# RWKV attention and two expert layers: r scaled in one piece, the diagonal term by transposed rows on TensorE, v loaded twice, decays on ScalarE, in the first two groups

## The chip, the cores and the metric

One core of a Trainium2 chip. The metric is device microseconds (us) of one execution; times of several runs of the kernel before: 460.25, 461.29 and 461.44, median 461.29. VectorE, ScalarE, GpSimd, TensorE and SyncE stand in the profile as DVE, ACT, POOL, PE and SP.

## What is computed

Three layers in a row, for 2 batches (B) of 768 tokens (S) of 384 values (8 heads H of D = 48). The change lies in the first, a linear attention with a state per head:

```python
def _attn_ref(r, k, v, w, u):
    B, H, S, D = r.shape
    state = np.zeros((B, H, D, D))
    for t in range(S):
        kt, vt, rt = k[:, :, t], v[:, :, t], r[:, :, t]
        cur = np.einsum('bhd,bhe->bhde', u[None] * kt, vt)
        y[:, :, t] = np.einsum('bhd,bhde->bhe', rt, state + cur)
        state = w[None, :, :, None] * state + np.einsum('bhd,bhe->bhde', kt, vt)
```

The term of `cur` (the diagonal term) is v of the same token times a coefficient, c = sum over d of r * u * k, one number per token and head. The second layer normalises each token and adds relu(x @ w_ch1) @ w_ch2 (384 to 1536 to 384). The third sends each token to one of 8 experts and multiplies with that expert's two matrices.

## The kernel before

**Groups.** Each batch is worked through in 6 groups g of 128 tokens. A group of batch b has the attention steps below; after them its tokens are normalised, transposed and pass the second layer's matmuls, and later routing to experts. Batch 1 goes a little ahead of batch 0 in the first two groups. After the sixth group the experts follow, one after another.

**An order written out by hand.** The string `ORDER` lists all steps; `name:engine.args` (p is POOL, d DVE, a ACT), for instance `kt:p.1.1` is step kt of batch 1, group 1 on GpSimd. The steps are issued in that order, so each engine, SyncE with its loads too, works through its own part of the list in order and waits wherever a step's input isn't there.

**Attention steps** of batch b, group g. Two blocks of 64 tokens (c = 0, 1) per group:
- `ld_T` (L256) loads r and k with heads' values on the partitions (r_, k_, 128 x 512); `ld_k` (L260) loads k with tokens on the partitions (kn_, 128 x 384); `ld_v` (L264) loads r that way (rn_), and v into two halves of the tile R.
- `kt` (L345) is k_ times powers of the decay; `L` (L348) is r_ times powers of it, for c = 0 and 1 in two calls of 64 partitions each; `knt` (L352) is kn_ times a table.
- `at` (at_pe, L383): 16 matmuls kt x L into a bank of PSUM; `am` (at_m, L391): on VectorE, two pieces, masks the result into L.
- The diagonal term: `rka` (L355) rn_ * u, `rkb` (L358) rn_ * kn_, `c` (L361) sums each head's 48 values (on ScalarE 8 pieces with an accumulator read each), `cv` (L369), in two halves, multiplies v (in R) with c.
- The state: `u` (u_pe, L398) 16 matmuls knt x v; `us` (u_s, L409) gives the state after the first block, a copy on ScalarE for group 0 and a sum on VectorE after; `uw` (L427) decays it; `ss` (s_s, L430) adds for the second block; `sw` (s_w, L433) decays that for the next group. `decayed` (L416) is one instruction on VectorE or GpSimd, and eight (one per head) on ScalarE.
- `y` (y_pe, L436): 16 matmuls; `yx` (y_x, L444) adds cv and sums; then `ym`, `yq`, `yr`, `ln` (L449 to L463) normalise (yr is on GpSimd always), `lt` (L466) transposes on TensorE, `lh` and `ll` (L471, L475) split the result into a high part and a residue.

**Weights of the second layer**, in the first stretch only: 12 chunks f. `ld_c.f` (L271) loads 768 KB into one of three tiles wq; `dec0`, `dec1`, `dec2` (L276 to L286) on VectorE decode a chunk to 32 bit; `w_g`, `w_hi` (L289, L294) on ScalarE scale it and round it to the high part, `w_lo` (L297) subtracts for the residue. With these, `m1.n` (mm1, L485) makes 18 matmuls for two chunks, `hh`, `hl` (L498, L501) take the relu apart on ScalarE and VectorE, `m2` (mm2, L508) makes 6 matmuls per batch. `SEQ` (L40) gives which two chunks m1.n needs: m1.0 the first two, m1.6 the last two (f = 10, 11).

Of the kernel before, what the change touches and what calls it, by code (L numbers as in the profile page):

```python
# [65 lines left out]
knt:d.1.3 yx.1.2 hh.11 rd.1.0 rl.0 hl.11 yr.0.2 knt:d.0.3 rm:d.0 m2.0.10 yq.1.2 yr.1.2 ln:p.0.2 rn.0 lt.0.2 rc.0 arg.0 ym:a.1.2
ln:p.1.2 lt.1.2 rkb:p.1.3 lh.0.2 lh.1.2 ll.0.2 m2.0.11 ll.1.2 ex.0 cv:p.0.3.0 L:p.0.3.1 x2.0.1 L:p.1.3.1 m2.1.11 x2.1.1 ld_v.0.4
row.0 m1.12 rr.0 hh.12 scan.0 col.0 L:d.1.3.0 oh.0 m1.13 hh.13 sum.0 hl.12 m2.1.12 rank.0 m1.14 pos.0 m2.0.12 c:d.1.3 hh.14
cv:p.0.3.1 hl.13 hl.14 m2.1.13 m2.0.13 ld_v.1.4 ld_k.1.4 m2.1.14 m2.0.14 sw:p.1.2 at.0.3 am.0.3 ld_T.0.4 cv:p.1.3.1 m1.15 hh.15
u.0.3 val.0 rw.0 tab.0 add.0 ld_k.0.4 m1.16 sw:a.0.2 us.0.3 hl.15 at.1.3 rka:p.0.4 m2.1.15 rt.0.1 uw:d.0.3 ss.0.3 y.0.3  # L70
rkb:p.0.4 c:a.0.4 ld_v.0.5 am.1.3 u.1.3 knt:p.1.4 yx.0.3 xs.0.1 us.1.3 uw:d.1.3 hh.16 yq.0.3 cv:p.0.4.1 re.0.1 ss.1.3 m1.17
xs.1.1 rt.1.1 y.1.3 hl.16 rd.0.1 re.1.1 ym:a.0.3 rd.1.1 m2.1.16 cv:p.1.3.0 yx.1.3 yq.1.3 hh.17 rka:d.0.5 hl.17 rl.1 m2.0.15
rm:a.1 rn.1 yr.0.3 sw:a.0.3 m2.0.16 ln:p.0.3 lt.0.3 rc.1 ym:p.1.3 arg.1 L:d.0.4.0 yr.1.3 ln:p.1.3 ld_T.1.4 L:p.1.4.1 lt.1.3
L:d.1.4.0 row.1 lh.0.3 lh.1.3 ll.0.3 rr.1 scan.1 ll.1.3 m2.1.17 x2.1.2 xs.1.2 m2.0.17 x2.0.2 rka:p.1.4 col.1 oh.1 m1.18 hh.18
L:d.0.4.1 hl.18 rank.1 m1.19 hh.19 sw:p.1.3 m2.1.18 rkb:p.1.4 pos.1 m2.0.18 hl.19 m2.1.19 ex.1 sum.1 val.1 m2.0.19 m1.20 c:d.1.4
ld_v.1.5 kt:d.0.4 hh.20 m1.21 rw.1 knt:p.0.4 hl.20 m2.0.20 ld_k.0.5 cv:d.0.4.0 m2.1.20 rkb:d.0.5 tab.1 hh.21 hl.21 kt:p.1.4
m2.1.21 c:a.0.5 ld_k.1.5 rka:p.1.5 rt.0.2 add.1 at.1.4 re.0.2 rd.0.2 am.1.4 rt.1.2 re.1.2 rd.1.2 cv:p.1.4.0 m2.0.21 cv:d.1.4.1
at.0.4 rl.2 rm:a.2 m1.22 am.0.4 u.0.4 hh.22 us.0.4 uw:p.0.4 u.1.4 rn.2 rc.2 ld_T.0.5 us.1.4 m1.23 hh.23 ss.0.4 y.0.4 kt:p.0.5
uw:d.1.4 ss.1.4 y.1.4 hl.22 hl.23 L:p.0.5.0 yx.0.4 yq.0.4 arg.2 ex.2 yx.1.4 yr.0.4 ym:d.0.4 L:d.0.5.1 ln:d.0.4 yq.1.4 ym:a.1.4
m2.0.22 row.2 rr.2 scan.2 m2.0.23 xs.0.2 x2.0.3 m2.1.22 lt.0.4 yr.1.4 ln:d.1.4 lt.1.4 lh.0.4 rkb:d.1.5 sum.2 lh.1.4 sw:p.1.4  # L80
m2.1.23 cv:p.0.5.1 ld_T.1.5 rt.0.3 col.2 ll.0.4 at.0.5 knt:p.1.5 x2.1.3 ll.1.4 m1.24 L:p.1.5.0 am.0.5 hh.24 hl.24 oh.2 m1.25
knt:p.0.5 re.0.3 m2.1.24 xs.1.3 rt.1.3 xs.0.3 rank.2 m1.26 u.0.5 cv:d.0.5.0 rd.0.3 hh.25 hl.25 val.2 re.1.3 L:p.1.5.1 rd.1.3
rl.3 pos.2 rw.2 tab.2 c:d.1.5 add.2 m2.1.25 hh.26 kt:p.1.5 at.1.5 m2.0.24 sw:p.0.4 us.0.5 am.1.5 y.0.5 rm:d.3 rn.3 rc.3 arg.3
u.1.5 m2.0.25 us.1.5 hl.26 row.3 yx.0.5 rr.3 scan.3 y.1.5 col.3 yq.0.5 m2.0.26 oh.3 rank.3 ym:a.0.5 cv:p.1.5.1 cv:p.1.5.0 yx.1.5
ym:a.1.5 yq.1.5 yr.0.5 ln:d.0.5 yr.1.5 ln:p.1.5 m1.27 lt.0.5 lh.0.5 pos.3 chp choose lt.1.5 lh.1.5 ll.0.5 m2.1.26 m1.28 ll.1.5
ldtop hh.27 hl.27 m2.1.27 ex.3 hh.28 hl.28 m2.0.27 m1.29 m2.0.28 sum.3 m2.1.28 hh.29 hl.29 m2.0.29 x2.0.4 m2.1.29 x2.1.4 rt.0.4
m1.31 re.0.4 val.3 rw.3 rd.0.4 xs.0.4 rt.1.4 m1.30 hh.31 hl.31 re.1.4 rd.1.4 rl.4 fill.4 fill.1 fill.3 hh.30 hl.30 fill.5 rm:a.4
fill.8 m1.33 rn.4 m1.32 rc.4 arg.4 row.4 m2.0.30 fill.6 hh.33 ex.4 sum.4 rr.4 scan.4 col.4 hl.33 tab.3 m2.1.30 oh.4 val.4 add.3
rank.4 pos.4 m2.0.31 fill.9 rw.4 m1.35 xs.1.4 hh.32 hl.32 fill.11 tab.4 fill.7 add.4 epc early eg.1 eg.0 m2.1.31 hh.35 fill.0
fill.10 m2.0.32 m1.34 m2.0.33 fill.2 lw.0 hh.34 hl.34 m2.1.32 hl.35 m2.0.34 m2.0.35 x2.0.5 m2.1.33 m2.1.34 etab m2.1.35 close  # L90
lw.1 x2.1.5 rt.0.5 re.0.5 ext.0 exh.0 rd.0.5 rt.1.5 xs.1.5 exl.0 re.1.5 rd.1.5 ext.1 exh.1 exl.1 rl.5 rm:d.5 e1.1 f0.2 f0.10
zX.0 rn.5 rc.5 arg.5 e1.0 row.5 f0.7 f0.1 f0.9 f0.8 f0.11 ex.5 sum.5 e1.2 e1h.1 e1l.1 rr.5 scan.5 col.5 e1h.0 e1l.0 oh.5 val.5
rank.5 pos.5 e1h.2 e1l.2 e1.3 e1h.3 e2.0.0 rw.5 e1l.3 pk finn tab.5 e2.0.1 add.5 fini f0.6 e2o.0 f0.4 f0.0 f0.3 xs.0.5 get.0.0
get.1.0 get.0.1 f0.5 f1.2 e2.1.0 e2.1.1 e2o.1 xt0.0 xh0.0 xl0.0 zX.1 f1.5 f1.0 lw.2 f1.1
f1.3 e2s.0 f1.4 e2s.1
# [1059 lines left out]
```

## Time and profile before

| | |
|---|---|
| median of three runs | 461.29 us (460.25 to 461.44) |
| the profiled execution's own time | 465.3 us |
| its span, first to last instruction | 463.4 us |
| busy: PE, DVE, POOL, ACT | 395.0, 308.5, 194.2, 186.3 us |
| mean granted clock of TensorE | 0.964 |

The rows used below come from views of one profiled execution. A row of stretches gives the stretch, its length, then per engine the busy us and the count of instructions (x), the granted clock (PEclk, share of full speed), the DMA engines' busy share and GB/s. A row of instructions in order of time gives start, length (of all, where several alike are merged as xN), engine, line, operation, output<-inputs, shape, and in brackets the idle time before it with what ended it. A row of groups gives the count, the summed busy us, the mean ns of one, and the idle before.

### The profile page before, as it was taken

The numbers are of one execution on the slowest core, as the hardware profiler recorded it, in microseconds if no ns is written. First come the engines' busy times: TensorE is split into PE (matmuls) and PEld (weight loads), VectorE is DVE, ScalarE is ACT, GpSimd is POOL, SyncE is SP. The second block draws the span as 40 slices with busy tenths as digits, with TensorE's granted clock in tenths as the row PEclk, the third lists the DMA queues.
The fourth block names the chain that finished last, engine by engine and source line by source line (L and its number), as shares of the span: only waits on it lengthen the run. The fifth ranks groups of instructions, "written<-read, shape, count | busy, mean of one in ns | idle before, by whom it ended". The sixth has DMA issues, their size and how long they took to land. (4 is left out here: it accounts for less than half of the span.)

```text
span 463.4 us, 8772 instructions
## 1 busy us (share of the span) xinstructions
PE 395.0 (85%) x3297; PEld 360.3 (78%) x3297; DVE 308.5 (67%) x606; ACT 186.3 (40%) x447; POOL 194.2 (42%) x252
## 2 busy tenths in 40 slices
...
GB/s 250 295 183 238 68 225 184 0 43 187 35 2 115 75 41 46 148 4 35 1 104 206 1 215 395 17 324 158 121 353 170 57 294 311 33 149 21 10 23 15
DMA packets 24849, 59.70 MB, mean 129 GB/s; under 512 B 3994, under 2 KB 10598, under 8 KB 24512
## 3 DMA queue, kind: packets, MB, share of 16 engines
...
q14 instruction: 43, 0.35, 0.2%
...
## 5 line engine op out<-in xcount | busy, mean ns | idle before, releaser
L514 PE MATMUL banks<-wh,H 128*128 128x384 f32 x288 | 84.9, 356 | 8.0 <-DVE H L502 6.5
L146 DVE TENSOR_TENSOR w2l<-wb,w2h 128x1024 fp32r<-128x1024 f32 (+1 forms) x33 | 33.1, 1028 | 52.9 <-ACT w2h L141 52.9
L514 PEld LDWEIGHTS banks<-wh,H 128*128 128x128 f32 x288 | 54.6, 196 | 10.3 <-DVE H L502 7.5
L973 PE MATMUL banks<-w1h,xq 128*128 128x512 f32 x168 | 58.3, 408 | 3.8 <-PEq L1060 2.8
L995 PE MATMUL banks<-w2h,H 128*128 128x384 f32 x224 | 48.2, 349 | 7.7 <-ACT H L141 7.7
L499 ACT ACTIVATE H<-banks 128x512 fp32r<-128x512 f32 x36 | 21.3, 594 | 78.7 <-PE banks L495 73.5
L514 PE MATMUL banks<-wl,H 128*128 128x384 f32 x144 | 50.0, 347 | 0.0
L995 PEld LDWEIGHTS banks<-w2h,H 128*128 128x128 f32 x224 | 40.9, 196 | 8.8 <-ACT H L141 8.2
L495 PE MATMUL banks<-xq,wh 128*128 128x256 f32 x216 | 44.7, 305 | 0.4 <-DVE xq L478 0.4
L973 PEld LDWEIGHTS banks<-w1h,xq 128*128 128x128 f32 x168 | 31.6, 188 | 13.6 <-issue 3.0
L495 PEld LDWEIGHTS banks<-xq,wh 128*128 128x128 f32 x216 | 36.8, 207 | 1.1 <-DVE xq L478 0.6
L502 DVE SCALAR_TENSOR_TENSOR H<-banks,H 128x512 fp32r<-128x512 f32 x36 | 24.5, 685 | 17.6 <-ACT H L499 17.5
L973 PE MATMUL banks<-w1l,xq 128*128 128x512 f32 x84 | 33.5, 398 | 0.2 <-DVEq L1060 0.2
L146 DVE TENSOR_TENSOR w1l<-wa,w1h 128x512 fp32r<-128x512 f32 (+1 forms) x36 | 32.5, 955 | 0.0
L495 PE MATMUL banks<-xq,wl 128*128 128x256 f32 x108 | 32.3, 299 | 0.0
L495 PE MATMUL banks<-xuh,wh 128*128 128x256 f32 x108 | 31.3, 290 | 0.0
L495 PE MATMUL banks<-xul,wh 128*128 128x256 f32 x108 | 30.6, 284 | 0.4 <-DVE xul L478 0.4
L495 PE MATMUL banks<-xuh,wl 128*128 128x256 f32 x108 | 30.5, 282 | 0.0
L141 ACT ACTIVATE w2h<-wb 128x1024 fp32r<-128x1024 f32 (+1 forms) x33 | 28.4, 902 | 3.2 <-DMA wb<-in_w 3.2
L372 POOL TENSOR_TENSOR cv<-R,c 64x384 f32<-64x384 f32 x19 | 18.8, 991 | 23.7 <-DVE c L367 22.0
L514 PEld LDWEIGHTS banks<-wl,H 128*128 128x128 f32 x144 | 28.2, 196 | 0.0
L141 ACT ACTIVATE w1h<-wa 128x512 fp32r<-128x512 f32 (+1 forms) x36 | 28.1, 855 | 0.0
...
## 6 DMA issues: line engine op xcount, KB each, us to landing
...
```

Source lines behind the costliest of these rows:

```text
L141: ACT.activation(out=dst_hi, in_=src, func=ACTF.Relu if relu else ACTF.Copy)
L146: (lo_eng or DVE).tensor_tensor(out=dst_lo, in0=src, in1=dst_hi.bitcast(F32), op=ALU.subtract)
L372: e.tensor_tensor(out=r3(cv[b][s], NH), in0=r3(R[b][g % 2][s, q, :], NH), in1=bc(c[s], [64, NH, HD]), op=ALU.mult)
L495: PE.matmul(out=ph[:, i, :], lhsT=a, rhs=x_[:, k, :], start=(q == 0), stop=(q == 8))
L499: ACT.activation(out=hh[:, ring(n)], in_=r3(B[3 + n % 2], 2), func=ACTF.Relu)
L502: DVE.scalar_tensor_tensor(out=hl[:, ring(n)], in0=r3(B[3 + n % 2], 2), scalar=0.0, in1=hh[:, ring(n)].bitcast(F32), op0=ALU.max, op1=ALU. ...
L514: PE.matmul(out=bank_o(b, g), lhsT=a[:, f2, s][:, i], rhs=w_[:, 2 * p + i, DM:], start=(p + i + n == 0), stop=(p == NP - 1 and i == 1 and ...
L973: PE.matmul(out=B[n], lhsT=a_[:, k, t], rhs=w_[:, k, n * 512:n * 512 + 512], start=(last == 0 and q == 0), stop=(last == 1 and q == KD - 1))
L995: PE.matmul(out=B[4][:, 0:DM], lhsT=a_[:, k, 0:128], rhs=w_[:, k, :], start=(q == 0), stop=(q == 23))
```

## The change

For groups 0 and 1 only: r times the powers is made in one piece (`Lr`, 128 partitions, into Ls); at_pe reads Ls, and ScalarE copies the two pieces that y_pe needs into L (`Lc`). The diagonal coefficient is made from the transposed rows: `rk` multiplies r_ by k_ in place, `cp` makes 16 matmuls of r_ with a column of u each, into the bank that at_pe used, and `cw` multiplies v with that column from PSUM. For that v is loaded into rn_ as well, in place of r. rka, rkb, c and cv of these groups go. All uw and sw of these groups are on ScalarE; w_lo, knt, kt, ln of the first stretch that stood on GpSimd are on VectorE, and five steps of group 2 as well (two L, two rka, one rkb; kt too). ld_un moves behind ld_v.0.1. Ls and two small tiles share the memory of x2. From cv.1.2.0 on the order is the old one. The order up to there and all other edits:

```diff
--- before.py
+++ after.py
@@ -33,7 +33,7 @@
 CAP = NTOK
 GATE_T = -1.5 * 2.0 ** -23
 BIG = float(1 << 20)
-C_ID, C_MK, C_RV, C_FT, C_JT, C_IO, C_TI, C_EO, C_JH, C_NC = 0, 128, 192, 200, 204, 220, 348, 360, 361, 385
+C_ID, C_MK, C_RV, C_FT, C_JT, C_IO, C_TI, C_EO, C_JH, C_UT, C_NC = 0, 128, 192, 200, 204, 220, 348, 360, 361, 385, 393
...
@@ -43,56 +43,55 @@
 
 ORDER = """
-zeros ld_wt zR:p.0.0 powers zR:p.1.0 ld_T.1.0 table kt:d.1.0 zR:p.0.1 ld_c.0 decay ld_cs L:d.1.0.1 L:d.1.0.0 zR:p.1.1 ld_gt wkc
-wkt wkn at.1.0 ld_T.0.0 L:p.0.0.1 ld_v.1.0 ld_un dec0.0 L:p.0.0.0 dec1.0 dec2.0 ld_k.1.0 knt:p.1.0 kt:d.0.0 ld_c.1 rka:d.1.0
-at.0.0 rkb:p.1.0 w_g.0 w_hi.0 w_lo:p.0 am.1.0 u.1.0 dec0.1 dec1.1 dec2.1 c:a.1.0 w_g.1 cv:d.1.0.1 ld_k.0.0 knt:p.0.0 w_hi.1
-us.1.0 am.0.0 ld_v.0.0 u.0.0 rka:p.0.0 rkb:d.0.0 c:a.0.0 us.0.0 uw:a.0.0 cv:p.1.0.0 ld_c.2 dec0.2 dec1.2 dec2.2 uw:d.1.0 ss.1.0
-y.1.0 w_g.2 ld_T.1.1 y.0.0 w_lo:p.1 ld_c.3 L:d.1.1.0 kt:p.1.1 yx.1.0 yq.1.0 ld_c.4 w_hi.2 cv:p.0.0.0 dec0.3 dec1.3 L:p.1.1.1
-cv:p.0.0.1 yx.0.0 yq.0.0 yr.1.0 at.1.1 ym:d.1.0 ym:p.0.0 ln:p.1.0 lt.1.0 yr.0.0 ln:p.0.0 ld_k.0.1 knt:p.0.1 dec2.3 ld_v.0.1
-w_lo:d.2 dec0.4 ss.0.0 dec1.4 dec2.4 w_g.3 w_hi.3 ld_v.1.1 lt.0.0 ld_k.1.1 lh.0.0 lh.1.0 w_g.4 w_hi.4 ll.0.0 w_lo:p.3 ld_T.0.1
-ll.1.0 L:p.0.1.1 u.0.1 m1.0 ld_c.5 kt:p.0.1 L:p.0.1.0 dec0.5 dec1.5 dec2.5 w_g.5 w_lo:d.4 rka:d.1.1 sw:p.0.0 ld_c.6 dec0.6
-rka:p.0.1 hh.0 rkb:p.0.1 dec1.6 w_hi.5 ld_c.7 hl.0 us.0.1 m1.1 hh.1 w_lo:p.5 dec2.6 hl.1 m2.0.0 m2.1.0 knt:p.1.1 dec0.7 dec1.7
-m2.0.1 dec2.7 uw:p.0.1 ss.0.1 w_g.6 ld_c.8 w_hi.6 w_lo:p.6 am.1.1 ld_c.9 dec0.8 m2.1.1 dec1.8 c:a.0.1 rkb:p.1.1 w_g.7 at.0.1
-am.0.1 w_hi.7 c:a.1.1 ld_c.10 m1.2 dec2.8 ld_k.1.2 w_g.8 hh.2 ld_k.0.2 w_lo:p.7 u.1.1 sw:p.1.0 m1.3 us.1.1 cv:p.1.1.0 cv:p.0.1.0
-hh.3 w_hi.8 cv:p.1.1.1 dec0.9 dec1.9 hl.2 y.1.1 yx.1.1 dec2.9 yq.1.1 ym:a.1.1 y.0.1 cv:p.0.1.1 yx.0.1 yq.0.1 uw:p.1.1 consts
-m2.1.2 hl.3 m2.0.2 w_g.9 w_hi.9 ym:d.0.1 m2.1.3 yr.1.1 ln:p.1.1 ss.1.1 lt.1.1 w_lo:d.8 yr.0.1 ln:d.0.1 dec0.10 ld_T.0.2 ld_c.11
-lt.0.1 lh.0.1 m2.0.3 kt:p.0.2 w_lo:d.9 m1.5 sw:d.1.1 lh.1.1 ll.0.1 ll.1.1 m1.4 dec1.10 dec2.10 ld_T.1.2 kt:p.1.2 hh.5 L:p.1.2.1
-hl.5 m2.1.5 m2.0.5 hh.4 dec0.11 w_g.10 w_hi.10 dec1.11 hl.4 m2.1.4 dec2.11 ld_v.0.2 w_g.11 rka:p.0.2 w_hi.11 rkb:p.0.2 m2.0.4
-L:p.0.2.1 c:d.0.2 m1.7 hh.7 ld_v.1.2 rka:p.1.2 rkb:d.1.2 w_lo:d.11 w_lo:p.10 m1.6 sw:d.0.1 hl.7 hh.6 hl.6 c:d.1.2 m2.0.7
-cv:p.1.2.0 ld_v.1.3 m2.1.7 m2.1.6 x2.1.0 xs.1.0 m2.0.6 x2.0.0 m1.8 hh.8 hl.8 L:p.1.2.0 xs.0.0 m1.9 hh.9 hl.9 cv:p.0.2.0
...
+zeros ld_wt zR:p.0.0 powers zR:p.1.0 ld_T.1.0 table kt:d.1.0 zR:p.0.1 ld_c.0 decay ld_cs Lr:d.1.0 zR:p.1.1 ld_gt wkc wkt wkn
+at.1.0 Lc.1.0.0 Lc.1.0.1 ld_T.0.0 Lr:d.0.0 ld_v.1.0 dec0.0 dec1.0 dec2.0 ld_k.1.0 knt:d.1.0 kt:d.0.0 ld_c.1 at.0.0 Lc.0.0.0
+Lc.0.0.1 rk:d.1.0 w_g.0 w_hi.0 am.1.0 cp.1.0 u.1.0 dec0.1 dec1.1 w_lo:d.0 dec2.1 w_g.1 ld_k.0.0 knt:d.0.0 w_hi.1 us.1.0 am.0.0
+ld_v.0.0 u.0.0 rk:d.0.0 cp.0.0 us.0.0 uw:a.0.0 cw:d.1.0 ld_c.2 dec0.2 dec1.2 dec2.2 uw:a.1.0 ss.1.0 y.1.0 w_g.2 ld_T.1.1 y.0.0
+w_lo:d.1 ld_c.3 Lr:d.1.1 kt:d.1.1 yx.1.0 yq.1.0 ld_c.4 w_hi.2 dec0.3 dec1.3 cw:d.0.0 yx.0.0 yq.0.0 yr.1.0 at.1.1 Lc.1.1.0
+Lc.1.1.1 ym:d.1.0 ym:d.0.0 ln:d.1.0 lt.1.0 yr.0.0 ln:d.0.0 ld_k.0.1 knt:d.0.1 dec2.3 ld_v.0.1 ld_un w_lo:d.2 dec0.4 ss.0.0
+dec1.4 dec2.4 w_g.3 w_hi.3 ld_v.1.1 lt.0.0 ld_k.1.1 lh.0.0 lh.1.0 w_g.4 w_hi.4 ll.0.0 w_lo:d.3 ld_T.0.1 ll.1.0 Lr:d.0.1 u.0.1
+m1.0 ld_c.5 kt:d.0.1 dec0.5 dec1.5 dec2.5 w_g.5 w_lo:d.4 sw:a.0.0 ld_c.6 dec0.6 hh.0 rk:d.0.1 dec1.6 w_hi.5 ld_c.7 hl.0 us.0.1
+m1.1 hh.1 w_lo:d.5 dec2.6 hl.1 m2.0.0 m2.1.0 knt:d.1.1 dec0.7 dec1.7 m2.0.1 dec2.7 uw:a.0.1 ss.0.1 w_g.6 ld_c.8 w_hi.6 w_lo:d.6
+am.1.1 ld_c.9 dec0.8 m2.1.1 dec1.8 rk:d.1.1 cp.1.1 w_g.7 at.0.1 Lc.0.1.0 Lc.0.1.1 am.0.1 cp.0.1 w_hi.7 ld_c.10 m1.2 dec2.8
+ld_k.1.2 w_g.8 hh.2 ld_k.0.2 w_lo:d.7 u.1.1 sw:a.1.0 m1.3 us.1.1 hh.3 w_hi.8 cw:d.1.1 dec0.9 dec1.9 hl.2 y.1.1 yx.1.1 dec2.9
+yq.1.1 ym:a.1.1 y.0.1 cw:d.0.1 yx.0.1 yq.0.1 uw:a.1.1 consts m2.1.2 hl.3 m2.0.2 w_g.9 w_hi.9 ym:d.0.1 m2.1.3 yr.1.1 ln:d.1.1
+ss.1.1 lt.1.1 w_lo:d.8 yr.0.1 ln:d.0.1 dec0.10 ld_T.0.2 ld_c.11 lt.0.1 lh.0.1 m2.0.3 kt:d.0.2 w_lo:d.9 m1.5 sw:a.1.1 lh.1.1
+ll.0.1 ll.1.1 m1.4 dec1.10 dec2.10 ld_T.1.2 kt:d.1.2 hh.5 L:d.1.2.1 hl.5 m2.1.5 m2.0.5 hh.4 dec0.11 w_g.10 w_hi.10 dec1.11 hl.4
+m2.1.4 dec2.11 ld_v.0.2 w_g.11 rka:d.0.2 w_hi.11 rkb:d.0.2 m2.0.4 L:d.0.2.1 c:d.0.2 m1.7 hh.7 ld_v.1.2 rka:d.1.2 rkb:d.1.2
+w_lo:d.11 w_lo:d.10 m1.6 sw:a.0.1 hl.7 hh.6 hl.6 c:d.1.2 m2.0.7 cv:p.1.2.0 ld_v.1.3 m2.1.7 m2.1.6 x2.1.0 xs.1.0 m2.0.6 x2.0.0
+m1.8 hh.8 hl.8 L:p.1.2.0 xs.0.0 m1.9 hh.9 hl.9 cv:p.0.2.0 rka:d.1.3 m2.1.8 m2.0.8 at.1.2 m2.1.9 rt.0.0 re.0.0 knt:p.1.2
...
@@ -264,7 +263,8 @@
         def ld_v(b, g):
             t0 = b * NS + g * 128
             Rt = R[b][g % 2]
-            SP.dma_start(out=rn_[b], in_=rn[t0:t0 + 128])
+
+            SP.dma_start(out=rn_[b], in_=(vn if g < 2 else rn)[t0:t0 + 128])
             SP.dma_start(out=Rt[0:64, 0, :], in_=vn[t0:t0 + 64])
             SP.dma_start(out=Rt[64:128, 1, :], in_=vn[t0 + 64:t0 + 128])
 
@@ -348,6 +348,29 @@
         def a_L(e, b, g, c):
             s = slice(64 - 64 * c, 128 - 64 * c)
             e.tensor_tensor(out=L[b][s, c], in0=r_[b][s], in1=Wr[s], op=ALU.mult)
+
+
+        def a_Lr(e, b, g):
+            e.tensor_tensor(out=Ls[b], in0=r_[b], in1=Wr, op=ALU.mult)
+
+        def a_Lc(b, g, c):
+            s = slice(64 - 64 * c, 128 - 64 * c)
+            ACT.activation(out=L[b][s, c], in_=Ls[b][s], func=ACTF.Copy)
+
+
+        def a_rk(e, b, g):
+            e.tensor_tensor(out=r_[b], in0=r_[b], in1=k_[b], op=ALU.mult)
+
+        def a_cp(b, g):
+            for h in range(NH):
+                for c in range(2):
+                    d = slice(64 * (1 - c), 64 * (1 - c) + HD)
+                    PE.matmul(out=bank_a(b, g)[64 * c:64 * c + 64, h:h + 1], lhsT=r_[b][d, h, :],
+                              rhs=cs[d, C_UT + h:C_UT + h + 1], start=True, stop=True)
+
+        def a_cw(e, b, g):
+            c = bank_a(b, g)[:, 0:NH].rearrange("p (h o) -> p h o", o=1)
+            e.tensor_tensor(out=r3(cv[b], NH), in0=r3(rn_[b], NH), in1=bc(c, [128, NH, HD]), op=ALU.mult)
 
         def a_knt(e, b, g):
             e.tensor_tensor(out=knt[b], in0=kn_[b], in1=Wkn, op=ALU.mult)
@@ -385,7 +408,8 @@
             for h in range(NH):
                 for c in range(2):
                     d0, s0 = 64 * (1 - c), 64 * c
-                    PE.matmul(out=pa[s0:s0 + 64, h, :], lhsT=kt[b][d0:d0 + HD, h, :], rhs=L[b][d0:d0 + HD, c, h, :],
+                    rhs = Ls[b][d0:d0 + HD, h, :] if g < 2 else L[b][d0:d0 + HD, c, h, :]
+                    PE.matmul(out=pa[s0:s0 + 64, h, :], lhsT=kt[b][d0:d0 + HD, h, :], rhs=rhs,
                               start=True, stop=True)
 
         def at_m(b, g):
@@ -531,7 +555,10 @@
 
             return B[7 * i if g == NG - 1 else (5, 1)[g % 2] + i]
 
-        x2 = [sm.tile([128, DM], F32, name=f"x2{b}") for b in range(NB)]
+
+        x2e = sm.tile([128, NB, 512], F32, name="x2e")
+        Ls = [r3(x2e[:, b], NH) for b in range(NB)]
+        x2 = [x2e[:, b, 0:DM] for b in range(NB)]
         x2T = sm.tile([128, 2, KD, NB, 128], F32R, name="x2T")
         lT = sm.tile([2 * (NE + 1), NB * 128], F32, name="lT")
         lg = sm.tile([128, NB, NE + 1], F32, name="lg")
@@ -540,7 +567,7 @@
         eq, dl, ex, q_ = (sm.tile(S8, F32, name=n) for n in ("eq", "dl", "ex", "q_"))
         fg = sm.tile([128, 2, NB], BF16, name="fg")
         f_ = sm.tile([128, NB], F32, name="f_")
-        ers = [sm.tile([NB, 128], F32, name=f"er{i}") for i in range(2)]
+        ers = [x2e[0:NB, i, DM:512] for i in range(2)]
         rr = lT[0:NB, 0:128]
         oh = sm.tile(S8, BF16, name="oh")
         ge = sm.tile([128, NB, JMAX + 1], F32, name="ge")
@@ -810,7 +837,7 @@
 
         tasks = dict(ld_wt=ld_wt, zR=zero_R, zeros=zeros, powers=powers, table=table, decay=decay, wkc=wkc, wkt=wkt, wkn=wkn, consts=consts, ld_cs=ld_cs, ld_un=ld_un, ld_gt=ld_gt,
                      ld_T=ld_T, ld_k=ld_k, ld_v=ld_v, ld_c=ld_c, dec0=dec0, dec1=dec1, dec2=dec2, w_g=w_g, w_hi=w_hi, w_lo=w_lo,
-                     kt=a_kt, L=a_L, knt=a_knt, rka=a_rka, rkb=a_rkb, c=a_c, cv=a_cv, at=at_pe, am=at_m, u=u_pe, us=u_s, uw=u_w, ss=s_s, sw=s_w,
+                     kt=a_kt, L=a_L, Lr=a_Lr, Lc=a_Lc, rk=a_rk, cp=a_cp, cw=a_cw, knt=a_knt, rka=a_rka, rkb=a_rkb, c=a_c, cv=a_cv, at=at_pe, am=at_m, u=u_pe, us=u_s, uw=u_w, ss=s_s, sw=s_w,
                      y=y_pe, yx=y_x, ym=y_m, yq=y_q, yr=y_r, ln=ln, lt=ln_pe, lh=ln_hi, ll=ln_lo, m1=mm1, hh=h_hi, hl=h_lo, m2=mm2,
                      x2=x2_add, xs=x2_st, rt=rt_t, re=rt_e, rd=rt_d, wgs=wg_split, rl=rt_l, rm=rt_lm, rn=rt_ln, rc=rt_lc, arg=rt_arg, ex=rt_ex, row=rt_row, rr=rt_rr,
                      scan=rt_scan, col=rt_col, oh=rt_oh, rank=rt_rank, pos=rt_pos, sum=rt_sum, val=rt_val, rw=rt_w, tab=rt_tab,
@@ -1118,6 +1145,9 @@
     cst[:, C_TI:C_TI + JMAX] = 1 + np.arange(NTOK).reshape(JMAX, 128).T
     cst[:, C_EO] = 128 * NE + np.arange(128)
     cst[:, C_JH:C_JH + HMAX] = 64 * np.arange(HMAX)
+    ut = np.zeros((2, 64, NH), f)
+    ut[:, :HD] = np.asarray(inputs["u"]).reshape(NH, HD).T
+    cst[:, C_UT:C_UT + NH] = ut.reshape(128, NH)
     import ml_dtypes
     p, q = np.arange(128)[:, None], np.arange(128)[None, :]
     cst_b = np.concatenate([(p < q), np.ones((128, 128)), np.eye(128)], axis=1).astype(ml_dtypes.bfloat16)
```

## Rows read from the trace of the kernel before

**Rows 1.** Stretches of the span, all engines.
```profile
50.00:60.00 10.00, 3.60 (x14) 3.08 (x13) 9.93 (x11) 3.92 (x10) 8.88 (x6) 0.73 0.29 88
100.00:130.00 30.00, 29.71 (x351) 27.45 (x350) 20.37 (x40) 7.78 (x23) 17.47 (x20) 1.00 0.32 102
```

**Rows 2.** Stretches, VectorE alone (busy, count, clock, DMA share, GB/s).
```profile
9.97:41.99 32.02, 31.30 (x33) 1.00 0.75 247
41.99:97.57 55.58, 51.84 (x54) 0.91 0.35 115
```

**Rows 3.** TensorE in order of time: first matmuls of m1.0, m1.1, m1.6, m2.0.7.
```profile
44.34 0.79 PE L495 MATMUL banks<-xq,wh 128*128 128x256 f32 x2
...
48.10 0.40 PE L495 MATMUL banks<-xq,wh 128*128 128x256 f32 x2
...
96.79 0.40 PE L495 MATMUL banks<-xq,wh 128*128 128x256 f32 x2
...
98.95 0.33 PE L514 MATMUL banks<-wh,H 128*128 128x384 f32 x1
```

**Rows 4.** VectorE and GpSimd in order of time.
```profile
17.20 1.81 POOL L298 TENSOR_TENSOR wl<-d,wh 128x768 fp32r<-128x768 f32 x1
17.51 1.91 DVE L277 TENSOR_SCALAR d<-wq 128x768 int32<-128x768 int32 x1
...
34.30 0.56 DVE L277 TENSOR_SCALAR d<-wq 128x768 int32<-128x768 int32 x1
34.89 0.96 DVE L281 SCALAR_TENSOR_TENSOR d<-wq,d 128x768 int32<-128x768 int32 x1
...
37.18 0.95 DVE L298 TENSOR_TENSOR wl<-d,wh 128x768 fp32r<-128x768 f32 x1
```

**Rows 5.** Stretch from 9.97 to 97.57, VectorE's instructions that read wq alone.
```profile
9.97:97.57 87.60, 50.67 (x36) 0.94 0.49 163
```

**Rows 6.** Groups on VectorE, 9.9 to 97.6 us, forms apart.
```profile
L396 DVE TENSOR_TENSOR L<-banks,cs 64x512 f32<-64x512 f32 x8 | 5.5, 688 | 0.2
...
L431 DVE TENSOR_TENSOR R<-ws,banks 48x384 f32<-48x384 f32 x4 | 2.2, 558 | 0.2
...
L346 DVE TENSOR_TENSOR kt<-k,Wk 128x512 f32<-128x512 f32 x1 | 0.7, 679 | 0.0
```

**Rows 7.** ScalarE and GpSimd in order of time.
```profile
29.31 1.91 ACT L421 ACTIVATE ws<-R,wC 48x48 f32<-48x48 f32 x8
31.23 0.99 ACT L292 ACTIVATE d<-d,gt_s 128x128 f32<-128x128 f32 x3
...
36.36 0.61 ACT L456 ACTIVATE xh<-x,sx 128x384 f32<-128x384 f32 x1 [0.50 <-DVE x L445]
...
38.31 0.84 ACT L295 ACTIVATE wh<-d 128x768 fp32r<-128x768 f32 x1
...
76.39 0.55 POOL L461 TENSOR_TENSOR rs<-rs,mhalf 128x1 f32<-128x1 f32 x1
...
88.87 0.60 ACT L499 ACTIVATE H<-banks 128x512 fp32r<-128x512 f32 x1 [2.26 <-PE banks L495]
```

**Rows 8.** SyncE's queue in order of time: ld_v.0.1 and ld_c.5 issued.
```profile
28.93 0.33 SPq L267 DMA_DIRECT2D rn<-in_rn  x1
...
33.87 0.38 SPq L272 DMA_DIRECT2D wq<-in_w_c  x1
```

**Rows 9.** The tile wq, 0 to 60 us: from a load's issue to its landing.
```profile
DMA to landing us min/median/max: 6.2/7.0/7.1
```

**Rows 10.** TensorE's bursts of 32 small matmuls in order of time (at, u, y, at).
```profile
9.99 1.98 PE L388 MATMUL banks<-L,kt 48*64 48x64 f32 x32 [0.19 <-DVE L L350]
...
20.33 1.52 PE L405 MATMUL banks<-R,knt 64*48 64x48 f32 x32 [1.62 <-POOL knt L353]
...
25.08 1.95 PE L441 MATMUL banks<-R,L 128*64 128x48 f32 x32 [2.85 <-ACT R L412]
...
63.27 1.15 PE L388 MATMUL banks<-L,kt 48*64 48x64 f32 x32
```

65 lines of the change are left out of this document (32 added, 33 removed).

## The prediction

> **What bounds the kernel now.** I read the stretches of the span first, all engines side by side. Between 50 and 60 us VectorE is busy for 9.93 of 10 us and TensorE for 3.60; between 100 and 130 us TensorE is busy for 29.71 of 30 [rows 1]. So the kernel has two halves: up to some 98 us VectorE's queue sets the pace, behind it TensorE does. All that this change touches lies in the first half. Then VectorE alone, from the first decode (dec0.0) to the end of the last weight residue there (w_lo.11): 31.30 + 51.84 = 83.1 us busy in 87.6, 4.5 us of waits [rows 2]. The first half ends for TensorE with m1.6, whose successor starts at 98.95 [rows 3]; it needs the last two decoded weight chunks. What m1.6 gains reaches the end of the kernel, as TensorE has next to no gap behind it.
>
> Next the instructions of VectorE in order of time. Its lengths are not those of its work: one decode takes 1.91 us while GpSimd runs a 768-wide subtraction (1.81 us), and the same instruction takes 0.56 us where GpSimd does little [rows 4]. That is where the change can earn.
>
> **Prices.** Times are those of the profiled execution (span 463.4, its own time 465.3, so 1.9 around it); the median of the runs is 461.29, and I carry a difference over unscaled. From the undisturbed rows: dec0 0.59 to the next start, dec1 0.96 and dec2 (the same form as dec1) 0.88, as an instruction that doesn't need its predecessor starts some 0.08 before that one's end: 2.46 a chunk; w_lo 0.88 [rows 4]. A 512-wide product with both inputs in SBUF 0.68, taken 0.61; a 384-wide one 0.56, so 0.48; at_m, two pieces of 0.69, 1.41; h_lo, as wide and also from PSUM, 0.60 [rows 6]. ScalarE: one decay (eight pieces) 1.91, w_g 0.99, w_hi 0.84, a relu 0.60, y_q 0.61 and about 0.2 for its accumulator; y_r on GpSimd about 0.8, of which 0.55 is the power [rows 7].
>
> **VectorE's work after.** GpSimd gives up seven w_lo, four knt, four kt, three ln and for group 2 two L, two rka and one rkb; the pairs L, rka, rkb, c, cv of groups 0 and 1 go, and Lr, rk, cw come. From dec0.0 to the end of w_lo.10 (now the last): 12 chunks x 2.46 = 29.5 (they take 50.7 now [rows 5]); 12 w_lo x 0.88 = 10.6; 4 at_m x 1.41 = 5.6; 13 products of 512 x 0.61 = 7.9; 6 h_lo x 0.60 = 3.6; 31 instructions of 384 x 0.48 = 14.9. Together 72.1 us in place of 83.1: 11 us less, with GpSimd's work taken in. cw reads one input in PSUM; I price it as the 384-wide sum that does so too [rows 6].
>
> **Its waits after.** I go down the new order with these prices from 10.0, where the first decode starts now [rows 2]; I take it unmoved, since Lr.0.0 in front of it waits for its load. (1) ss.1.0 comes due at 24.2; its decay uw.1.0 on ScalarE stands behind w_g.1, w_hi.1, two copies (0.5 each, less than a relu) and uw.0.0, which begin when dec2.1 ends at 18.9: 25.4, a wait of 1.2. (2) ln.0.0 waits for y_q and y_r: 1.0. m1.0 can start at 40.2, against 44.34 now [rows 3]. (3) dec0.5, due at 41.4, waits for its load: SyncE issued it at 33.87, 4.94 after ld_v.0.1 [rows 8]; ld_v.0.1 now waits for cw.0.0, which ends at 30.5, and ld_un stands in between, so 30.5 + 4.94 + 0.5 = 35.9, landing 6.2 to 7.1 later [rows 9]: 42.1 to 43.0, taken 42.3, a wait of 0.9. (4) hl.0 waits for hh.0 behind w_g.5 and sw.0.0 on ScalarE: 0.7. rk.1.1 then ends at 59.65.
>
> Here stands the chain that decides. In TensorE's order come cp.1.1 (needs rk.1.1), at.0.1, cp.0.1 (needs am.0.1, since the coefficients go into the bank that am.0.1 reads) and only then m1.2; before, at.0.1 and m1.2 stood there with no VectorE instruction between them. On the way: cp 1.0, at 1.98, am 1.41, cp 1.0, m1.2 3.76, hh.2 0.7, and behind it on ScalarE the decay sw.1.0, 1.91. us.1.1 on VectorE needs sw.1.0: 59.65 + 11.8 = 71.4. (5) am.0.1 waits 3.0 for at.0.1; (6) us.1.1 waits 5.6, as only dec2.8 and w_lo.7 stand between. Queued behind us.1.1 are the decodes 9 to 11. (7) ss.1.1 waits 1.55 for uw.1.1, behind y_q; (8) ll.1.1 waits 0.95, as lh.1.1 stands behind sw.1.1.
>
> Sum of the waits 14.9 in place of 4.5: 10.0 + 72.1 + 14.9 = 97.0 for the end of w_lo.10. m1.6 reads that chunk with its third matmul of 18, pitch 0.12 (2.16 us for all [rows 3]): 97.0 + 1.9 = 98.9, against 98.95. **Nearly the whole 11 us turns into waits.** I put the gain at 0.1 us.
>
> **The cp price, and the clock.** cp is 16 matmuls with 64 stationary columns and one moving column; no row has that form. Bursts of 32: 64 stationary and 64 moving 1.98 us, 64 and 48 1.95, 48 and 48 1.52 [rows 10]. It goes by the stationary columns, so 16 x 0.062 = 1.0; the lower bound is the burst of 1.15 at the faster clock, 0.58 [rows 10]. The Trainium skill, page "TensorE: Matmul & The Clock Gate", section "Wait — 56ns, not 53.3ns?", says that start-to-start doesn't fall below about 25 ns however few columns move: by it a cp could take 0.4 (an estimate), and the two on the chain 1.2 less, 460.0 in all. The same burst shape at two lengths is the two levels of the clock, 1.2 and 2.4 GHz; m1.0 after a quiet stretch takes 3.76, m1.6 2.16 [rows 3], and in 50 to 60 us with TensorE busy for 3.60 the granted clock was 0.73 on average [rows 1]. Before cp.1.1 TensorE stands idle for some 4.5 us, so I take the lower level for the whole chain.
>
> **At nothing** I cost: v loaded in place of natural r (the same bytes); Lc on ScalarE, which stands behind at_pe there and ahead of weights that VectorE takes later (cover gone: 2 x 0.6 a group); the removed c on ScalarE, which nobody waited for long; GpSimd's rest, idle until cv.1.2.0, which follows c.1.2 after hl.6 as before. C_NC grows by 8 columns: nothing.
>
> **Rivals.** (a) *The clock stays up* over that gap: cp 0.42 less twice, at 0.83, m1.2 1.60, together 3.3, all of it on the chain: 457.9. For it: the m2 matmuls end only shortly before. Against: [rows 1, 3] as above. (b) *The early waits don't come*: (1) and (2) vanish since ScalarE is quicker through its queue; all after it hangs on rk.1.1, so 2.2 less: 459.0; with (3) and (4) 457.4. (c) *cp is short*: 0.58 each, by the lower bound, gives 460.4. (The Trainium skill's figure above gave 460.0.) (d) *Slower, by VectorE's own pace*: if its instructions, now fed by more engines, don't overlap, each of the some 75 up to rk.1.1 costs up to 0.08 more; half of that is 3.0, the early waits absorb about 1.0: 463.2. It decides where rk.1.1 ends after 61.0. (e) *GpSimd was not what stretched VectorE*: the decodes stay at 50.7 in place of 29.5: 21 more, 482. Against it stand the short decodes of [rows 4].
>
> **How the numbers follow.** Forecast 461.2, chance 0.39; (a) 0.18, (b) 0.15, (c) 0.05, (d) 0.19, (e) 0.04. A measurement here tells some 0.3%, 1.4 us, from no change. Faster are (a) and (b): 0.33; slower (d) and (e): 0.23; the forecast and (c) lie within: 0.44. The range takes in (b) whole and (a) with a short cp, and above (d) with the load of (3) landing at 43.0 (0.7 more): 457.0 to 463.8. The forecast's own range is 460.0 to 462.5.
>
> **What would show it.** Right: decodes of 0.56, 0.96 and 0.95 all through the first 97 us; VectorE busy for about 72 us there with some 15 idle; TensorE idle in front of cp.1.1, and m1.2 starting at about 65; VectorE's longest wait ahead of us.1.1, released by sw.1.0. Each step is wrong where its wait is missing; the clock row between 60 and 69 tells (a). Wrong as a whole: decodes above 1.2 us, or m1.6 over 1.4 us from 98.9.

## The result and the profile after

The changed kernel takes 466.56 us (median, 465.91 to 466.89) against 461.37 (460.25 to 461.88) for the kernel before in the same comparison: ratio 1.0103, 95% interval 1.0075 to 1.0132. It is 1% slower. Ratios here and below leave out slow executions, over 1.5% above the fastest of their kernel; medians and ranges are of all. The forecast was no change, 461.2, with a range up to 463.8; the result lies outside it, on the side of rival (d).

The profiled execution of after took 465.91 us, span 464.1. The one of before had taken 465.3, 4 us above its own median, so the two spans differ by 0.7 only. The place to compare is therefore the end of the first half. Four rows of TensorE and VectorE, in order of time: m1.6's third matmul, the first matmul of m2.0.7 (98.95 before [rows 3]), the last two weight residues, and the first sum of the second layer's output, which I call x2.1.0.

```profile
101.04 0.39 PE L519 MATMUL banks<-xq,wl 128*128 128x256 f32 x1 [1.09 <-DVE wl L298]
...
103.05 0.34 PE L538 MATMUL banks<-wh,H 128*128 128x384 f32 x1
...
99.17 1.82 DVE L298 TENSOR_TENSOR wl<-d,wh 128x768 fp32r<-128x768 f32 x2
...
106.43 0.56 DVE L542 TENSOR_TENSOR x2e<-banks,x 128x384 f32<-128x384 f32 x1 [1.40 <-PE banks L538]
```

The same sum in the trace of before:

```profile
102.28 0.56 DVE L518 TENSOR_TENSOR x<-banks,x 128x384 f32<-128x384 f32 x1 [1.34 <-PE banks L514]
```

m1.6 ends 4.1 us later and x2.1.0 starts 4.15 later, and TensorE's wait there is for VectorE's residue (w_lo.10), which ends at 100.99 where I had put 97.0. So the 4 us are lost before 101 us, in the stage that the change touches.

VectorE in stretches from its first decode, cut at the end of rk.1.1 and at the start of us.1.1 (busy us, count, clock, DMA share, GB/s), to be read against [rows 2]:

```profile
10.40:61.04 50.64, 46.12 (x71) 0.99 0.68 228
61.04:74.86 13.82, 3.21 (x6) 0.56 0.36 113
74.86:100.99 26.13, 22.80 (x40) 0.87 0.14 43
sum 90.59, DVE 72.14; mean DVE 24.05
```

VectorE is busy for 72.1 us, as forecast, and idle for 18.45 instead of 14.9. Of these 18.45, 1.3 are gaps of at most 0.11 us between one instruction and the next, which the forecast, priced from start to start, meant to have in its 72.1. Most of the idle time stands in the middle stretch, where VectorE is busy for 3.21 of 13.82 us and the granted clock is 0.56. VectorE's groups from 10.4 to 101 us, forms apart, show the decodes (12 each) and the residues:

```profile
L281 DVE SCALAR_TENSOR_TENSOR d<-wq,d 128x768 int32<-128x768 int32 x12 | 11.5, 957 | 0.3
L285 DVE SCALAR_TENSOR_TENSOR d<-wq,d 128x768 int32<-128x768 int32 x12 | 11.5, 955 | 0.2
L298 DVE TENSOR_TENSOR wl<-d,wh 128x768 fp32r<-128x768 f32 x12 | 11.3, 952 | 0.1
L277 DVE TENSOR_SCALAR d<-wq 128x768 int32<-128x768 int32 x12 | 6.7, 554 | 0.8 <-DMA wq<-in_w_c 0.7
```

36 decodes now take 29.6 us; they took 50.7 [rows 5]. What eats the gain is this chain, in order of time on TensorE, VectorE and ScalarE (cp.1.1, at.0.1, am.0.1, cp.0.1, the first two matmuls of m1.2 and its last, hh.2, sw.1.0, us.1.1):

```profile
61.10 1.87 PE L368 MATMUL banks<-cs,r 48*64 48x1 f32 x32 [6.11 <-DVE r L362]
62.82 1.95 PE L412 MATMUL banks<-x2e,kt 48*64 48x64 f32 x32
...
64.82 1.39 DVE L420 TENSOR_TENSOR L<-banks,cs 64x512 f32<-64x512 f32 x2 [3.78 <-PE banks L412]
...
66.27 1.87 PE L368 MATMUL banks<-cs,r 48*64 48x1 f32 x32 [1.49 <-DVE L L420]
68.07 0.80 PE L519 MATMUL banks<-xq,wh 128*128 128x256 f32 x2
...
71.86 0.41 PE L519 MATMUL banks<-xq,wl 128*128 128x256 f32 x1
...
72.31 0.60 ACT L523 ACTIVATE H<-banks 128x512 fp32r<-128x512 f32 x1 [4.09 <-PE banks L519]
72.94 1.89 ACT L445 ACTIVATE ws<-R,wC 48x48 f32<-48x48 f32 x8
...
74.86 0.55 DVE L438 TENSOR_TENSOR R<-ws,banks 48x384 f32<-48x384 f32 x1 [6.78 <-ACT ws L445]
```

Each step starts within 0.2 us of the end of the one above. VectorE waits 3.78 us ahead of am.0.1 and 6.78 ahead of us.1.1, and the decodes 9 to 11 queue behind.

### The profile page after: what moved, and what is told of

Its sections match the earlier page's. It is cut to its first block, busy times and chain, and to the rows that moved or that the text cites. A ratio compares the mean times of both kernels' runs of the same rounds, so it can differ in the third digit from the quotient of the medians.

```text
span 464.1 us, 8981 instructions
## 1 busy us (share of the span) xinstructions
PE 402.0 (87%) x3425; PEld 367.1 (79%) x3425; DVE 294.7 (64%) x632; ACT 197.5 (43%) x447; POOL 130.1 (28%) x207
## 5 line engine op out<-in xcount | busy, mean ns | idle before, releaser
L538 PE MATMUL banks<-wh,H 128*128 128x384 f32 x288 | 83.0, 349 | 2.5 <-ACT H L523 1.5
L538 PEld LDWEIGHTS banks<-wh,H 128*128 128x128 f32 x288 | 53.1, 190 | 4.5 <-ACT H L523 1.7
L519 PE MATMUL banks<-xq,wh 128*128 128x256 f32 x216 | 47.1, 315 | 2.3 <-DVE xq L502 2.3
L538 PE MATMUL banks<-wl,H 128*128 128x384 f32 x144 | 48.9, 339 | 0.0
L519 PEld LDWEIGHTS banks<-xq,wh 128*128 128x128 f32 x216 | 38.6, 216 | 3.2 <-DVE xq L502 2.8
L519 PE MATMUL banks<-xq,wl 128*128 128x256 f32 x108 | 33.3, 308 | 1.1 <-DVE wl L298 1.1
L484 POOL TENSOR_SCALAR rs<-sq 128x1 f32<-128x1 f32 x12 | 2.9, 238 | 80.8 <-ACT nm L475 55.0
```

Of the source, the lines that this page charges most:

```text
L484: POOL.tensor_scalar(out=rs[b], in0=sq[b], scalar1=float(DM) ** -3, scalar2=1e-6, op0=ALU.mult, op1=ALU.add)
L519: PE.matmul(out=ph[:, i, :], lhsT=a, rhs=x_[:, k, :], start=(q == 0), stop=(q == 8))
L538: PE.matmul(out=bank_o(b, g), lhsT=a[:, f2, s][:, i], rhs=w_[:, 2 * p + i, DM:], start=(p + i + n == 0), stop=(p == NP - 1 and i == 1 and ...
```

## The experiments

In the texts below, theory A is: the loss is this chain, made by the two cp in TensorE's queue ahead of m1.2. In most of these kernels the lines stand one or more further down (L439 is L438 of after), because the order's text is longer. Runs of the kernel before that were taken between them ranged from 460.1 to 469.8, so each kernel is read by its ratio to them.

**e1: the two cp behind m1.3.** Nothing between needs them; cw.1.1 is the first reader.

```diff
-dec1.8 rk:d.1.1 cp.1.1 w_g.7 at.0.1 Lc.0.1.0 Lc.0.1.1 am.0.1 cp.0.1 w_hi.7
+dec1.8 rk:d.1.1 w_g.7 at.0.1 Lc.0.1.0 Lc.0.1.1 am.0.1 w_hi.7
...
-u.1.1 sw:a.1.0 m1.3 us.1.1
+u.1.1 sw:a.1.0 m1.3 cp.1.1 cp.0.1 us.1.1
```

> Edit: the changed kernel with cp.1.1 and cp.0.1 moved behind m1.3 in the order. Theory A (the added wait is TensorE's order: rk.1.1, cp.1.1, at.0.1, am.0.1, cp.0.1 stand in line ahead of m1.2): at.0.1 follows m2.1.1 at about 55 us, m1.2 starts before 60 in place of 68, VectorE's wait of 3.8 us ahead of am.0.1 vanishes, us.1.1 starts at about 67 in place of 74.9, and the kernel takes 457.5 to 460. Theory B (TensorE's lower clock between 60 and 70, granted 0.50, is what costs): the order gives little, at most 2 us, 464.5. Theory C (the decays on ScalarE are what costs): us.1.1 still waits for sw.1.0, which stands behind w_g.8 and hh.2; less than 4 us gained, above 462.5.

Measured: 461.01 (456.64 to 463.07), ratio 0.9961 (0.9921 to 1.0000). TensorE (at.0.1), then VectorE in order of time (us.1.1 and cw.1.1):

```profile
56.21 1.15 PE L413 MATMUL banks<-x2e,kt 48*64 48x64 f32 x32
...
68.16 0.55 DVE L439 TENSOR_TENSOR R<-ws,banks 48x384 f32<-48x384 f32 x1 [2.57 <-ACT ws L446]
...
69.16 0.56 DVE L374 TENSOR_TENSOR cv<-rn,banks 128x384 f32<-128x384 f32 x1 [0.45 <-PE banks L369]
```

us.1.1 starts 6.7 us earlier than in after, am.0.1 doesn't wait, and x2.1.0 starts at 100.95 instead of 106.43. The move of two TensorE steps takes the loss away, as A says, though the time lies 1 us above A's range and us.1.1 still waits 2.57 us for sw.1.0. at.0.1 now follows m2.1.1 at once and takes 1.15 us instead of 1.95: with the new place of the cp the lower level of the clock is gone there too, so this run alone doesn't part the order from the clock; e6 does.

**e2: only the decay sw.1.0 earlier on ScalarE**, to test whether ScalarE's decays are the cause.

```diff
-cp.0.1 w_hi.7 ld_c.10 m1.2
+cp.0.1 w_hi.7 sw:a.1.0 ld_c.10 m1.2
...
-u.1.1 sw:a.1.0 m1.3
+u.1.1 m1.3
```

> Edit: the changed kernel with sw.1.0 moved on ScalarE ahead of w_g.8 and hh.2, the TensorE order as changed. Theory A: us.1.1 then waits for u.1.1, which TensorE makes after m1.2; it starts at about 73.0 in place of 74.9, and the kernel takes about 464.7. Theory C: sw.1.0 is done by 61, us.1.1 starts at about 68, and the kernel takes 460 or less. Theory B: as A, within 1 us.

Measured: 466.41 (465.25 to 468.03), ratio 1.0090 (1.0046 to 1.0134), as after within the noise and 1.7 us above what A gave. us.1.1 waits nearly as long, now for u.1.1, which stands behind m1.2 on TensorE:

```profile
73.94 0.55 DVE L439 TENSOR_TENSOR R<-ws,banks 48x384 f32<-48x384 f32 x1 [5.77 <-PE banks L430]
```

ScalarE's decay is one end of the chain and not its cause: without it the loss stays.

**e3: both.**

```diff
-dec1.8 rk:d.1.1 cp.1.1 w_g.7 at.0.1 Lc.0.1.0 Lc.0.1.1 am.0.1 cp.0.1 w_hi.7 ld_c.10 m1.2
+dec1.8 rk:d.1.1 w_g.7 at.0.1 Lc.0.1.0 Lc.0.1.1 am.0.1 w_hi.7 sw:a.1.0 ld_c.10 m1.2
...
-u.1.1 sw:a.1.0 m1.3 us.1.1
+u.1.1 m1.3 cp.1.1 cp.0.1 us.1.1
```

> Edit: both moves. Theory A: us.1.1 waits only for VectorE's own queue and u.1.1, at about 64 to 65; the last residue w_lo.10 ends near 92 in place of 101, and the kernel takes 456 to 458, faster than the kernel before the change (461.4). Theory B: not below 463. Theory C: no better than the move of sw.1.0 alone.

Measured: 459.99 (456.14 to 462.65), ratio 0.9934 (0.9891 to 0.9976). It is faster than before, but by less than A said, and w_lo.10 ends at 95.6, not near 92. us.1.1 has no wait any more; it came back one instruction later, ahead of cw.1.1, since the cp now stand behind m1.3, and m1.3 waits for a residue of VectorE (TensorE, then VectorE, in order of time):

```profile
66.14 0.39 PE L520 MATMUL banks<-xq,wl 128*128 128x256 f32 x1 [3.55 <-DVE wl L299]
...
69.19 0.56 DVE L374 TENSOR_TENSOR cv<-rn,banks 128x384 f32<-128x384 f32 x1 [2.52 <-PE banks L369]
```

x2.1.0 starts at 100.99, as in e1. My reading was that the place of the cp in e1 is itself too late; e7 tries an earlier one.

**e4: 18 steps back on GpSimd** (seven w_lo, four knt, four kt, three ln), the rest as in after.

```diff
-w_lo:d.0
+w_lo:p.0
...
-knt:d.1.0
+knt:p.1.0
...
-ln:d.1.0
+ln:p.1.0
```

> Edit: the changed kernel with seven w_lo, four knt, four kt and three ln of the first stretch put back on GpSimd, nothing else. Theory P (GpSimd's two-input work stretches VectorE's): the mean of a decode instruction goes from 0.82 us back to 1.2 to 1.4 us, VectorE is busy for longer in the first 100 us although it has 18 instructions less, and the kernel is slower than the changed one, 468 to 472. Rival (GpSimd doesn't stretch it): decodes stay at 0.82 us, VectorE is freed of some 13 us, and the kernel takes 460 or less.

Measured: 470.69 (468.29 to 471.9), ratio 1.0206 (1.0145 to 1.0268). The decodes, in groups on VectorE:

```profile
L286 DVE SCALAR_TENSOR_TENSOR d<-wq,d 128x768 int32<-128x768 int32 x12 | 13.3, 1107 | 0.3
L282 DVE SCALAR_TENSOR_TENSOR d<-wq,d 128x768 int32<-128x768 int32 x12 | 13.1, 1092 | 0.3
L278 DVE TENSOR_SCALAR d<-wq 128x768 int32<-128x768 int32 x12 | 9.7, 808 | 3.8 <-DMA wq<-in_w_c 2.5 <-POOL wl L299 1.1
```

Their mean is 1.00 us (36.1 over 36) against 0.82 in after and 1.41 before. The time is the expected one; the mean has risen as expected, but to less than the 1.2 to 1.4 that I gave. In the order of the change, then, having these 18 steps off GpSimd is worth some 1.1%. Which of them count is not shown, and 1.1 us of VectorE's waits here are for a residue of GpSimd itself.

The next four were run together, beside one set of runs of the kernel before (median 463.73).

**e5: after, unchanged**, in more rounds.

> The changed kernel as it is, timed again beside the kernel before on this chip. Theory A (5 us lost to the new order): 466 to 468, above the kernel before by 3 to 6 us. Rival N (the difference is the spread of executions, which for the kernel before reached from 460 to 470 us): the two medians within 1.4 us.

Measured: 467.59 (464.63 to 469.31), ratio 1.0093 (1.0060 to 1.0127); the loss is no accident of the first comparison. us.1.1 waits 6.25 us for sw.1.0 and x2.1.0 starts at 107.52.

**e6: TensorE kept busy in the gap**, with 40 extra matmuls ahead of cp.1.1 and 10 behind at.0.1 into a bank that nothing reads there; the order of the work is that of after.

```diff
+def warm(n):
+    for q in range(n):
+        PE.matmul(out=B[7][:, 0:256], lhsT=wh[:, 0, 0:128], rhs=XT[0][0][:, 0, :], start=True, stop=True)
...
-rk:d.1.1 cp.1.1 w_g.7 at.0.1 Lc.0.1.0
+rk:d.1.1 warm.40 cp.1.1 w_g.7 at.0.1 warm.10 Lc.0.1.0
```

> Edit: the changed kernel, its order kept, with 40 extra matmuls of 256 columns into a bank not in use while TensorE stands idle ahead of cp.1.1, and 10 between at.0.1 and cp.0.1. Their result is not used. Theory B (the lower clock has a share): the granted clock is 1.00 between 60 and 70 us in place of 0.50; cp takes 0.95 in place of 1.87, at 1.15 in place of 1.98, m1.2 2.2 in place of 3.8; us.1.1 starts at 70.5 in place of 74.9, and the kernel takes 4 us less than the changed one, about 462.5. Theory A without a share of the clock: us.1.1 at 74 or later, 466.

Measured: 464.06 (461.38 to 471.34), ratio 0.9999 (0.9961 to 1.0037), where e5 has 1.0093: 0.9% less, some 4 us. All engines between 60 and 70 us, in after and then in e6:

```profile
60.00:70.00 10.00, 7.41 (x105) 7.21 (x106) 4.25 (x6) 0.99 (x3) 0.00 (x0) 0.50 0.18 49
```

```profile
60.00:70.00 10.00, 8.89 (x166) 8.42 (x167) 4.15 (x6) 2.90 (x10) 0.00 (x0) 1.00 0.42 134
...
61.00 1.10 PE L369 MATMUL banks<-cs,r 48*64 48x1 f32 x32 [1.31 <-DVE r L363]
...
70.60 0.55 DVE L443 TENSOR_TENSOR R<-ws,banks 48x384 f32<-48x384 f32 x1 [4.23 <-ACT ws L450]
...
102.12 0.56 DVE L547 TENSOR_TENSOR x2e<-banks,x 128x384 f32<-128x384 f32 x1 [1.35 <-PE banks L543]
```

The granted clock is 1.00 instead of 0.50, the upper of the two levels, 2.4 GHz, instead of 1.2. The same cp takes 1.10 us instead of 1.87, and us.1.1 starts 4.3 us earlier than in after. It still waits 4.23: the chain is there at either level, the lower one makes it longer. x2.1.0 (the last row) starts at 102.12, where before has 102.28, and the time is that of before. So the loss against before takes both, the order and the lower level behind the idle stretch that the order makes: with the same order at the upper level it is gone. Another order of the same steps gains on top of that, as e7 shows.

**e7: a better place for everything on the chain.** The cp right behind m1.2 (not m1.3), sw.1.0 behind w_hi.7, uw.1.1 behind w_hi.8.

```diff
-dec1.8 rk:d.1.1 cp.1.1 w_g.7 at.0.1 Lc.0.1.0 Lc.0.1.1 am.0.1 cp.0.1 w_hi.7 ld_c.10 m1.2 dec2.8
+dec1.8 rk:d.1.1 w_g.7 at.0.1 Lc.0.1.0 Lc.0.1.1 am.0.1 w_hi.7 sw:a.1.0 ld_c.10 m1.2 cp.1.1 cp.0.1 dec2.8
...
-u.1.1 sw:a.1.0 m1.3 us.1.1 hh.3 w_hi.8 cw:d.1.1
+u.1.1 m1.3 us.1.1 hh.3 w_hi.8 uw:a.1.1 cw:d.1.1
```

> Edit: the changed kernel with cp.1.1 and cp.0.1 behind m1.2, sw.1.0 ahead of w_g.8 and uw.1.1 right behind w_hi.8 on ScalarE. Theory A: cw.1.1 no longer waits 2.5 us for cp, ss.1.1 no longer 1.7 us for uw.1.1; w_lo.10 ends 3 to 4 us earlier than with the two moves alone (that ran at 460.0), and the kernel takes 456 to 457.5. Rival: TensorE is the bound there by now, and less than 1 us is gained.

Measured: 457.87 (456.74 to 459.75), ratio 0.9889 (0.9850 to 0.9928). It beats both kernels: 1.1% below before, 2.1% below after (457.87 over 467.59), and lies 0.4 us above what A gave. As uw.1.1 was moved too, what it gains over e3 isn't parted between the two moves. TensorE in order of time (at.0.1, m1.2, the two cp) and us.1.1 on VectorE:

```profile
55.28 1.15 PE L413 MATMUL banks<-x2e,kt 48*64 48x64 f32 x32
56.35 0.51 PE L520 MATMUL banks<-xq,wh 128*128 128x256 f32 x2
...
61.45 3.26 PE L369 MATMUL banks<-cs,r 48*64 48x1 f32 x58 [2.68 <-DVE r L363]
...
66.11 0.55 DVE L439 TENSOR_TENSOR R<-ws,banks 48x384 f32<-48x384 f32 x1 [1.43 <-PE banks L430]
```

at.0.1 and m1.2 follow on m2.1.1 without a gap and run at the upper level (1.15 where after has 1.95), and TensorE's wait for rk.1.1, 2.68 us, now stands behind them (the cp after it still run at the lower level's pace, 3.26 us for 58 records). us.1.1 starts 8.75 us earlier than in after, x2.1.0 at 97.44, 9 earlier.

**e8: the moves between engines without the new arithmetic.** The order and arithmetic of before; 48 steps of the first stretch change engine: w_lo, knt, kt, L, rka, rkb, cv, ln and ym from GpSimd to VectorE, uw and sw to ScalarE.

> Edit: the kernel before, its order and its arithmetic, with the steps of the first stretch off GpSimd (w_lo, knt, kt, L, rka, rkb, cv, ln, ym on VectorE, uw and sw on ScalarE) as the change has them. Theory P plus A: decodes of 0.56 and 0.96 us, VectorE busy for about 79 us in the first stretch, no cp between at.0.1 and m1.2, so m1.2 starts at about 60; the kernel takes 458 to 463, faster than the changed one by over 3 us: the moves off GpSimd alone are no loss. Rival (VectorE can't carry it): its first stretch ends later than 100 us, 466 or more.

Measured: 464.41 (462.61 to 466.69), ratio 1.0030 (1.0004 to 1.0056), a little above what I expected. The decodes are as short as in after (0.553, 0.958 and 0.956 us), but VectorE carries rka, rkb and cv as well: 78.5 us busy between 10 and 100 us, against 75.6 in e7. us.1.1 still waits 2.58 for sw.1.0, and x2.1.0 starts at 105.56, 3.3 us later than in before. So the moves alone, in the order and arithmetic of before, gain nothing. This kernel has no cp on its chain and is 3.2 us below e5 all the same.

**e9: the kernel before, traced again.**

> The kernel before, unchanged, profiled again. Theory A (before's first trace ran some 3 us late behind the stage that the change touches, which its timed runs mostly don't): the first sum of the second layer's output (x2.1.0 on VectorE) starts at 102.3 within 0.7 again, and the span lies nearer to 459.5 than to 463.4; then the 4 us between the two kernels at x2.1.0 are the whole difference of the medians. Rival S (the first trace is before's own pace throughout): x2.1.0 at 102.3 too, but the span is 463.4 within 1, and only 1 us of the 5 is explained by the traces.

Measured: 465.79 with a span of 463.9 and x2.1.0 at 102.54. The span went against A: both traced executions of before (465.3 and 465.79) lie above the medians of its runs (461.29 to 463.74). Part of it has a place. The later sums at L518 that open at 132.44 and 174.80 in the first trace (132.72 and 175.07 in this one) stand 42.4 us apart, those of after 40.2 (136.65 and 176.88), and just ahead of the second one the granted clock has fallen in before:

```profile
170.00:175.00 5.00, 4.58 (x16) 4.16 (x17) 4.94 (x7) 0.27 (x1) 2.90 (x3) 0.66 0.00 0
```

In after it is 1.00 in the answering stretch, 169 to 177 us. So the traces give back 2.1 of the 4.15 us there; that the level of the clock is what costs before these 2.1 us was not tested. Whether the runs without a trace do so is open; their medians differ by 5.2 us (first comparison) and 3.9 (e5).

## Why the prediction was wrong

**The failed step is the price of cp**: "it goes by the stationary columns, so 16 x 0.062 = 1.0". I divided a burst row marked x32 by 32 and multiplied by the 16 matmuls of a cp. But a step at is written as 16 matmuls too, and its row has x32 [rows 10]: each of these fp32 matmuls leaves two records. So 1.98 was the price of one whole step of 16, and a cp costs as much: 1.87 in the profile, with its successors starting 1.72 and 1.80 us after it. Two cp cost 3.52 where I had 2.0: 1.5 us, all on the chain. The listing of the kernel and the row's own count would have told me. The bounds fell with it: 0.58 was half of a burst, and its whole, 1.15, lies above the price that I took; at the upper level e6 measured 1.10. By the floor of about 25 ns between starts in the Trainium skill, page "TensorE: Matmul & The Clock Gate", section "Wait — 56ns, not 53.3ns?", I had a cp at 0.4. With 32 records in place of 16 it would be 0.8 (an estimate); in e6 the next step starts 0.95 us after cp.1.1, 30 ns a record, which agrees with the floor: it was the count that I had wrong.

**The rest is lateness on the same chain.** rk.1.1 ends at 61.04, forecast 59.65. The first decode starts at 10.40 instead of 10.0. VectorE is busy for 46.1 us up to there, and 0.9 more go into gaps of under 0.1 us between its instructions: 47.0 where I had 45.9, as more of them than I took start behind their predecessor's end. The other waits are 3.6 instead of 3.8, among them one that I had not seen (0.52 at yx.0.0, for cw.0.0 right in front of it). m1.2 from first start to last end is 4.2, not 3.76: that was the distance from m1.0's first start to the next step's [rows 3], and hh.2 waits for the last end. Together rk.1.1 1.4 late, the chain 13.8 instead of 11.8, and from us.1.1 to the end of w_lo.10 26.1 instead of 25.6: 4.0 us, which is what m1.6 lost. The price of cp is the largest term of these, but not all: put right by itself, it gives 462.7, still inside the range. All of them together give 465.2; the last 1.4 us to 466.56 have no place in the traces.

**The structure held.** The listed waits, forecast and measured:

| wait | forecast | after |
|---|---|---|
| (1) ss.1.0 | 1.2 | 0.84 |
| (2) ln.0.0 | 1.0 | 1.01 |
| (3) load of dec0.5 | 0.9 | 0.70 |
| (4) hl.0 | 0.7 | 0.52 |
| (5) am.0.1 | 3.0 | 3.78 |
| (6) us.1.1 | 5.6 | 6.78 |
| (7) ss.1.1 | 1.55 | 1.72 |
| (8) ll.1.1 | 0.95 | 1.27 |

VectorE's busy time (72.1), its decodes, the place of the longest wait and its releaser, and the lower level of the clock were right. So was the refusal of rival (a): the granted clock was 0.50. Rival (e) falls with the short decodes. Rival (d) named the right sign, and rk.1.1 did end after its mark of 61.0, by 0.04 us. Its mechanism has a share, VectorE's own pace, but 1.1 us of it where (d) had 3.0. The late start (0.4) and the unforeseen wait (0.5) helped it past the mark, and the longer chain it did not name. My balance was also struck between unlike things: the 4.5 us of waits before hold 1.4 of small gaps, my 14.9 after held none. And the ends of the range don't follow from the cases that they name, whose times are 457.4 and 463.9; the result lies outside either way. What I should have weighed is that an exact balance (11 us less work, 10.4 more waits) leaves the sign to errors on one chain without slack, and that every unforeseen thing on it can only make it longer. My rival for "slower" was given 0.19 and the smaller part of the reason.

**What the change is worth.** Less GpSimd work shortens the decodes (e4: undoing it costs 1.1%, the difference of the ratios 1.0206 and 1.0093). The cp ahead of m1.2 cost 1.3 to 1.4%: the ratio is 0.9961 with them behind m1.3 (e1) and 1.0093 to 1.0103 with them ahead. The cost is in the order, with the level of the clock that it brings (e6), and not in the arithmetic: with the same steps in the order of e7 the change is 1.1% faster than before.
